# Softplus from ScalarE's softplus table instead of abs, exp, ln and four VectorE operations, in a linear attention followed by a softplus MLP

## The chip, the cores and the metric

One core of one Trainium2 chip. The core has TensorE (PE, with weight loads shown apart as PEld), VectorE (DVE), ScalarE (ACT), GpSimd (POOL) and SyncE (SP, which only issues DMAs here). Each engine takes its instructions in the order of its own queue; semaphores order the engines against each other. The metric is the time on the device in microseconds (us), the median of several runs.

## The reference

```
kv  = einsum('bhsd,bhse->bhde', k, v)            # 8 batches, 8 heads, 576 tokens, 64 features
out = einsum('bhsd,bhde->bhse', q, kv)
rms = sqrt(mean(out * out, axis=-1) + 1e-06)
x   = (out / rms * g_norm), as 4608 tokens x 512 features
h   = x @ w_in                                   # 512 x 2048
g   = maximum(h, 0) + log1p(exp(-abs(h)))        # softplus
y   = g @ w_out                                  # 2048 x 512, float32
```

q, k and v are float32. w_in and w_out come as float64 and are rounded to float32 on the core.

## The kernel before

The tokens are worked in 12 blocks of 384. A block has 16 slots, one for each 128 of the 2048 hidden features; slots are counted on through the blocks here, so slot 16 is the first of block 1. What a slot holds is written out by hand, and each engine's queue has that order.

*mm1* (lines 236 to 258), once per slot: four float32 matmuls into a PSUM tile hp of 128x384, then softplus into g, the block's tile of hidden activations. There are two hp buffers, so the hp of a slot can start when the softplus two slots earlier has read its hp for the last time. The softplus is three ScalarE operations (L249 Abs, L250 Exp, L252 Ln) and four VectorE operations (L254, L255, L256, L257). L256 is the last that reads hp; L257 writes g.

*mm2* (262 to 273), in 12 of the 16 slots of the next block: a quarter (four matmuls) of op = g^T w_out for 128 tokens; after the last quarter ScalarE copies the result out and it is stored.

*The attention* of batch b is dealt over slots. stage_turn (171) has the transposes of q (tp), which ScalarE (L187) and VectorE (L189) copy out, and the product kv (L192), copied by L194 and L195. stage_out (203) forms o, its squares on ScalarE (L211) and x times g_norm on VectorE (L212). stage_squares (215) sums the squares by a matmul (ss), which VectorE brings to ms (L220). stage_root (223) is one ScalarE square root per batch, with a load of ScalarE's table ahead of it and another after it (L225). stage_norm (227), eight per batch, is a VectorE reciprocal (L229) and a product (L231). All PSUM tiles of the attention come from one pool of four buffers.

*The conversion* of the weights (convert, 119) goes in 32 chunks, each a 128x512 piece: 16 of w_in, then 16 of w_out. Six are converted during the first batch, 26 in slots 0 to 15, one or two per slot. A chunk takes one ScalarE operation (L132, c_lf), five on VectorE (L133 c_h, L134 and L136 c_t, L138 c_p, L141 c_m) and four on GpSimd (L139 c_m from c_h, L143, L144 and L147, tensor-tensor operations, the last of which writes the weight). VectorE's L141 waits for GpSimd's L139 of the same chunk, and GpSimd's L139 waits for VectorE's L133. The buffers between them are double, so c_lf of a chunk waits until GpSimd has done with the chunk two before it.

*Order in a slot.* In slots 0 to 15 each engine's queue has the slot's mm1 with its softplus first, then the attention of batch 1 that falls on the slot, then the slot's conversion. Batch 1 has its turns, outs and squares in slots 0 to 8, its root in slot 8 and one norm in each of slots 8 to 15. From slot 16 on, the later batches' attention stands between mm1 and mm2.

*Memory.* The conversion's buffers are given back after block 0, and the second g tile (g1, for the odd blocks) is placed there (lines 312 to 315). So the first write of g1, in slot 16, waits for the end of the conversion.

Of the kernel before, what the change touches and what calls it, by code (L numbers as in the profile page):

```python
# [8 lines left out]
F32 = mybir.dt.float32  # L9
U32 = mybir.dt.uint32  # L10
AF = mybir.ActivationFunctionType
ALU = mybir.AluOpType
PSUM = bass.MemoryType.PSUM

P = 128
# [4 lines left out]
def kernel(  # L20
# [7 lines left out]
    moe_w_out: bass.AP,  # L28
    out: bass.AP,
):  # L30
    """Per batch and pair of heads: kv = k^T v, x^T = kv^T q^T (features on partitions, so that it is
    the moving operand of the next product), the mean of squares over a head by a product with a
    block of ones, which leaves it on every row of the head. Then per block of NT tokens:
    g = softplus(w_in^T x^T), out = g^T w_out. Products and sums are float32; weights that come as
    float64 (their bits in 64-bit integers) are rounded to it here. The attention of the batches
    ahead is dealt out over the slots of the block products."""
    nc = tc.nc
    B, H, S, D = q.shape
    d_model, d_ff = moe_w_in.shape
    n_tokens = out.shape[0]  # L40
    assert (B, H, S, D, d_model) == (8, 8, 576, 64, 512) and n_tokens == B * S
    NP = H // 2                      # pairs of heads
    KD, KF = d_model // P, d_ff // P
    J = 6                            # tokens on one partition of q, k and v
    R = S // J                       # partitions of q, k and v
    HS = S // 2                      # half of a batch's tokens: one bank of PSUM
    JH = J // 2
    NT = 384                         # tokens of a block
    SLOTS = KF
    GB = 2                           # batches whose x^T lies in one tile  # L50
    BPT = GB * S // NT               # blocks of such a tile
    n_blocks = n_tokens // NT

    ctx.enter_context(tc.manual_schedule())
# [12 lines left out]
    block = const.tile([P, P], F32, name="block")  # L67
# [5 lines left out]
    def load(u):  # L73
        if u >= B * NP:
            return
        b, p = divmod(u, NP)
        tiles = []
        for n, src in (("q", q), ("k", k), ("v", v)):
            # q and k are stationary operands: the pair's 128 features lie together for each j
            t = qkv.tile([R, 2, J, D] if n == "v" else [R, J, 2, D], F32, tag=n, name=f"{n}_t")  # L80
            pair = src[b, 2 * p:2 * p + 2].rearrange("h (r j) d -> r h j d", j=J)
            if n == "v":
                nc.sync.dma_start(out=t, in_=pair)
            else:
                for e in range(2):
                    nc.sync.dma_start(out=t[:, :, e], in_=pair[:, e])
            tiles.append(t)
        loaded[u] = tiles
# [3 lines left out]
    conv_pool = tc.tile_pool(name="conv", bufs=2)  # L92
    conv = conv_pool.__enter__()
    raws = {}
    CHUNKS = 2 * KF                  # a weight's columns (w_in) or rows (w_out) of one kf

    def weight(c):
        """DRAM and SBUF views of chunk c, d_model values on a partition."""
        kf = c % KF
        if c < KF:  # L100
            words = moe_w_in.bitcast(U32) if wide else moe_w_in
            n = words.shape[1] // KF
            return (words[:, kf * n:(kf + 1) * n].rearrange("(a p) f -> p a f", p=P),
                    w_in_t[:, :, kf * P:(kf + 1) * P])
        words = moe_w_out.bitcast(U32) if wide else moe_w_out
        return words[kf * P:(kf + 1) * P].rearrange("(a p) f -> p a f", p=P), w_out_t[:, kf:kf + 1]
# [10 lines left out]
            out=raws[c].rearrange("p n two -> p (n two)").rearrange("p (a f) -> p a f", a=src.shape[1]), in_=src)  # L117

    def convert(c):
        """float64 -> float32, from the words hi (sign, exponent, 20 bits of mantissa) and lo.  # L120

        t: hi's value in float32: the exponent's top bit and its low seven stay, the three between
        only tell the range. p: t's power of two with its sign. So the value is t + lo 2^-52 p,
        which one addition rounds. m is 1 inside float32's normal range, 0 below it, huge above."""
        if not wide:
            return
        raw = raws.pop(c)
        lo, hi = raw[:, :, 0], raw[:, :, 1]
        t, p, h = (conv.tile([P, d_model], U32, tag=n, name=f"c_{n}") for n in "tph")
        lf, m = (conv.tile([P, d_model], F32, tag=n, name=f"c_{n}") for n in ("lf", "m"))  # L130
        tf, pf = t.bitcast(F32), p.bitcast(F32)
        nc.scalar.activation(lf, lo, func=AF.Copy, scale=2.0 ** -52)  # L132
        nc.vector.tensor_scalar(out=h, in0=hi, scalar1=0x7FFFFFFF, scalar2=None, op0=ALU.bitwise_and)  # L133
        nc.vector.tensor_scalar(out=t, in0=hi, scalar1=3, scalar2=0x3FFFFFF8,  # L134
                                op0=ALU.logical_shift_left, op1=ALU.bitwise_and)
        nc.vector.scalar_tensor_tensor(out=t, in0=hi, scalar=0xC0000000, in1=t,  # L136
                                       op0=ALU.bitwise_and, op1=ALU.bitwise_or)
        nc.vector.tensor_scalar(out=p, in0=t, scalar1=0xFF800000, scalar2=None, op0=ALU.bitwise_and)  # L138
        nc.gpsimd.tensor_scalar(out=m, in0=h, scalar1=float((1023 + 128) << 20), scalar2=3e38,  # L139
                                op0=ALU.is_ge, op1=ALU.mult)  # L140
        nc.vector.scalar_tensor_tensor(out=m, in0=h, scalar=float((1023 - 126) << 20), in1=m,  # L141
                                       op0=ALU.is_ge, op1=ALU.add)
        nc.gpsimd.tensor_tensor(out=lf, in0=lf, in1=pf, op=ALU.mult)  # L143
        nc.gpsimd.tensor_tensor(out=lf, in0=lf, in1=tf, op=ALU.add)  # L144
        _, dst = weight(c)
        a = dst.shape[1]
        nc.gpsimd.tensor_tensor(out=dst, in0=lf.rearrange("p (a f) -> p a f", a=a),  # L147
                                in1=m.rearrange("p (a f) -> p a f", a=a), op=ALU.mult)
        fetch(c + 3)
# [5 lines left out]
    for c in range(3 if wide else CHUNKS):  # L155
        fetch(c)

    nc.scalar.preload_act_table_set("natural_log_exp_and_others")
    ln_one = const.tile([P, 1], F32, name="ln_one")
    nc.vector.memset(ln_one, 0.0)  # L160
    nc.scalar.activation(ln_one, ln_one, func=AF.Ln, bias=1.0)
    make_identity(nc, ident)
    for t in [block] + kv_diag:
        nc.vector.memset(t, 0.0)
# [4 lines left out]
    qTs, sqs = {}, {}  # L169

    def stage_turn(u):
        """q^T and the block-diagonal kv of a pair of heads."""
        b, p = divmod(u, NP)
        if p == 0:
            mss[b] = att.tile([P, 2, NP, HS], F32, tag="ms", bufs=1, name="ms")
# [25 lines left out]
        return xTs[b // GB][:, p, c:c + HS]  # L201

    def stage_out(u):
        """The attention's rows times g, and their squares."""
        b, p = divmod(u, NP)
        qT = qTs.pop(u)
        for h in range(2):
# [14 lines left out]

    def stage_root(b):
        nc.scalar.activation(mss[b], mss[b], func=AF.Sqrt)  # L224
        nc.scalar.preload_act_table_set("natural_log_exp_and_others")  # L225

    def stage_norm(b, h, p):
        r = mss[b][:, h, p]
# [7 lines left out]
    def mm1(n, kf):  # L236
# [5 lines left out]
        for kd in range(KD):  # L242
            nc.tensor.matmul(hp, lhsT=w_in_t[:, kd, kf * P:(kf + 1) * P], rhs=xT[:, kd, c:c + NT],  # L243
                             start=(kd == 0), stop=(kd == KD - 1))
        # softplus(h) = max(h, 0) + log1p(u), u = exp(-|h|);
        # log1p(u) = ln(w) + (u - (w - 1)) with w = 1 + u rounded, which keeps small u whole
        # once what the table gives for ln(1) is taken off.
        u = tmp.tile([P, NT], F32, tag="u", name="u")
        nc.scalar.activation(u, hp, func=AF.Abs)  # L249
        nc.scalar.activation(u, u, func=AF.Exp, scale=-1.0)  # L250
        ln = tmp.tile([P, NT], F32, tag="ln", name="ln")
        nc.scalar.activation(ln, u, func=AF.Ln, bias=1.0)  # L252
        w = tmp.tile([P, NT], F32, tag="w", name="w")
        nc.vector.tensor_scalar(out=w, in0=u, scalar1=1.0, scalar2=None, op0=ALU.add)  # L254
        nc.vector.scalar_tensor_tensor(out=w, in0=w, scalar=1.0, in1=u, op0=ALU.subtract, op1=ALU.subtract)  # L255
        nc.vector.scalar_tensor_tensor(out=ln, in0=hp, scalar=0.0, in1=ln, op0=ALU.max, op1=ALU.add)  # L256
        nc.vector.scalar_tensor_tensor(out=gs[n][:, kf], in0=ln, scalar=ln_one, in1=w,  # L257
                                       op0=ALU.subtract, op1=ALU.subtract)

    PARTS = 4                        # slots over which one tile of 128 tokens is summed  # L260

    def mm2(n, i, part):
        if part == 0:
# [8 lines left out]
            r0 = n * NT + i * P  # L272
            nc.sync.dma_start(out=out[r0:r0 + P], in_=ot)

    # the first batch
    for t in range(NP + 2):
        if t < NP:
            stage_turn(t)
# [7 lines left out]
        for p in range(NP):  # L286
            stage_norm(0, h, p)

    # the other batches, by slot
    agenda = {}  # L290

    def at(slot, f, *a):
        agenda.setdefault(slot, []).append((f, a))

    for b in range(1, B):
        # the slot where the first block that takes from batch b starts, less the slots of its work
        due = (b * S // NT) * SLOTS
        s0 = max(due - (28 if b % GB else 30), 0)
        for p in range(NP):
# [4 lines left out]
        for i in range(2 * NP):  # L304
            at(s0 + 2 * NP + (i + 1 if b > 1 else i), stage_norm, b, i // NP, i % NP)

    AHEAD = NP + 2                   # chunks of the weights that are ready before the first block
    for c in range(AHEAD, CHUNKS):
        at((c - AHEAD) * SLOTS // (CHUNKS - AHEAD), convert, c)

# [44 lines left out]
```

## Time and profile before

| | us |
|---|---|
| median of 3 runs (lowest, highest) | 1355.65 (1354.22, 1356.6) |
| profiled execution, span | 1353.7 |
| PE busy in the span | 1166.8 (86%) |
| VectorE busy | 775.3 (57%) |
| ScalarE busy | 418.8 (31%) |
| GpSimd busy | 214.2 (16%) |

The page of the profile gives each engine's busy time in 40 equal slices, in tenths, and the clock that PE was granted (PEclk, in tenths of full speed). A row of the timeline gives the start, the duration in us, the engine, the line, the operation with its output and inputs, and in brackets how long the engine stood idle before it and which operation ended that wait. A row of the waits gives who waited for whom, us in total, the number of times and the longest. The lines are those of the kernel before.

### The profile page before, as it was taken

What the parts mean: (1) busy time and instruction counts of PE and PEld (TensorE: products, weight loads), DVE (VectorE), ACT (ScalarE), POOL (GpSimd) and SP (SyncE); (2) the same over time, 40 slices, a digit from 0 to 9 for tenths busy, and PEclk for the clock granted to TensorE, in tenths of its full rate; (3) what the DMA queues carried; (4) which work ended last, traced back from release to release, by engine and by line L of the source; (5) the groups of instructions that cost most, each with busy time, mean ns of one, the idle gap of its engine ahead of it and who ended that gap; (6) DMA issues with size and microseconds to landing.
All of it is one profiled execution on the core that took longest, in us unless ns stands there. A gap on an engine that the chain in (4) does not pass through costs nothing.

```text
span 1353.7 us, 10306 instructions
## 1 busy us (share of the span) xinstructions
PE 1166.8 (86%) x3520; PEld 642.1 (47%) x3520; DVE 775.3 (57%) x1254; ACT 418.8 (31%) x798; POOL 214.2 (16%) x134
## 2 busy tenths in 40 slices
PE   6164524259999999999999999999999999999998
PEld 4042312125555555555555555555555555555543
DVE  4888989885384476343674584335844754343320
ACT  2222222113433343333432433334233333233320
POOL 5658776770000000000000000000000000000000
PEclk8667766579999999999999999999999999999999
DMA  9324311102202200012012100121020000000000
GB/s 212 86 73 115 89 62 46 62 16 66 55 8 61 61 8 8 16 46 68 16 35 60 35 9 8 30 65 35 8 61 9 8 16 9 8 8 8 16 8 24
DMA packets 98582, 55.21 MB, mean 41 GB/s; under 512 B 77536, under 2 KB 91872, under 8 KB 98528
## 3 DMA queue, kind: packets, MB, share of 16 engines
q1 hardware_dynamic: 98528, 54.54, 14.9%
q8 instruction: 28, 0.46, 0.1%
q14 instruction: 26, 0.21, 0.0%
HBM read 45.09 MB, written 9.44 MB: 40 GB/s over the span
## 4 chain that ended last, share of the span: by engine, by line
PE 76%; DVE 10%; POOL 8%; ACT 3%; issue 1%; DMA 1%; SPq 1%; POOLq 0%; ACTq 0%
PE op L267 36%; PE hp L243 34%; POOL c_m L139 4%; PE kv L192 3%; DVE ms L229 2%; PE o L209 2%; DVE w L255 2%; DVE w L254 2%; POOL c_lf L143 2%; POOL c_lf L144 1%; DVE g L257 1%; DVE c_m L141 1%; ACT qT L187 1%; ACT u L250 1%; ACT u L249 1%
## 5 line engine op out<-in xcount | busy, mean ns | idle before, releaser
L243 PE MATMUL hp<-xT,w_in_t 128*128 128x384 f32 x1536 | 550.7, 507 | 111.3 <-DVE ln L256 85.2
L267 PE MATMUL op<-w_out_t,g 128*128 128x512 f32 x1152 | 516.1, 592 | 0.0
L243 PEld LDWEIGHTS hp<-xT,w_in_t 128*128 128x128 f32 x1536 | 303.7, 199 | 358.4 <-issue 98.6
L254 DVE TENSOR_SCALAR w<-u 128x384 f32<-128x384 f32 x192 | 85.9, 448 | 468.1 <-ACT u L250 468.1
L267 PEld LDWEIGHTS op<-w_out_t,g 128*128 128x128 f32 x1152 | 217.0, 190 | 238.1 <-issue 211.9
L249 ACT ACTIVATE u<-hp 128x384 f32<-128x384 f32 x192 | 93.9, 489 | 580.5 <-PE hp L243 580.4
L257 DVE SCALAR_TENSOR_TENSOR g<-ln,ln_one,w 128x384 f32<-128x384 f32 x192 | 124.9, 650 | 14.5 <-POOL w_out_t L147 0.7
L255 DVE SCALAR_TENSOR_TENSOR w<-w,u 128x384 f32<-128x384 f32 x192 | 122.3, 637 | 6.7
L229 DVE RECIPROCAL ms<-ms 128x288 f32<-128x288 f32 x64 | 124.5, 1945 | 2.2 <-ACT ms L224 2.2
L256 DVE SCALAR_TENSOR_TENSOR ln<-hp,ln 128x384 f32<-128x384 f32 x192 | 105.9, 551 | 0.9
L252 ACT ACTIVATE ln<-u 128x384 f32<-128x384 f32 x192 | 100.5, 524 | 6.1
L250 ACT ACTIVATE u<-u 128x384 f32<-128x384 f32 x192 | 100.4, 523 | 6.1
L139 POOL TENSOR_SCALAR c_m<-c_h 128x512 f32<-128x512 uint32 x32 | 70.4, 2201 | 81.7 <-DVE c_h L133 80.6
L192 PE MATMUL kv<-v_t,k_t 96*128 96x128 f32 x384 | 58.7, 310 | 21.6 <-ACT qT L187 16.2
L192 PEld LDWEIGHTS kv<-v_t,k_t 96*128 96x128 f32 x384 | 52.7, 217 | 26.6 <-ACT qT L187 20.6
L132 ACT ACTIVATE c_lf<-raw 128x512 f32<-128x512 uint32 x32 | 21.2, 667 | 127.3 <-POOL w_out_t L147 84.7
L209 PE MATMUL o<-qT,kv_diag 128*128 128x288 f32 x128 | 40.8, 445 | 21.1 <-DVE kv_diag L195 20.4
L143 POOL TENSOR_TENSOR c_lf<-c_lf,c_p 128x512 f32<-128x512 f32 x32 | 56.5, 1767 | 2.6
L271 ACT COPY ot<-op 128x512 f32<-128x512 f32 x36 | 21.1, 586 | 109.1 <-PE op L267 109.1
L184 PE MATMUL tp<-ident,q_t 96*128 96x96 f32 x192 | 24.3, 266 | 24.9 <-DVE xT L212 18.9
L209 PEld LDWEIGHTS o<-qT,kv_diag 128*128 128x128 f32 x128 | 25.8, 207 | 34.1 <-DVE kv_diag L195 22.3
L219 PE MATMUL ss<-sq,block 128*128 128x288 f32 x128 | 37.7, 419 | 4.4 <-DVE xT L212 2.9
(33 smaller groups left out, 469.9 us busy)
## 6 DMA issues: line engine op xcount, KB each, us to landing
q_t<-in_q_dram SPq DMA_DIRECT2D x64, 144.0 KB, 3.1
k_t<-in_k_dram SPq DMA_DIRECT2D x64, 144.0 KB, 3.5
v_t<-in_v_dram SPq DMA_DIRECT2D x32, 288.0 KB, 3.8
out_dram<-ot SPq DMA_DIRECT2D x36, 256.0 KB, 2.0
raw<-in_moe_w_in_dram SPq DMA_DIRECT2D x16, 512.0 KB, 4.1
raw<-in_moe_w_out_dram SPq DMA_DIRECT2D x16, 512.0 KB, 3.3
g_col<-in_g_norm_dram SPq DMA_DIRECT2D x2, 0.2 KB, 3.1
```

Source lines behind the costliest of these rows:

```text
L139: nc.gpsimd.tensor_scalar(out=m, in0=h, scalar1=float((1023 + 128) << 20), scalar2=3e38, op0=ALU.is_ge, op1=ALU.mult)
L192: nc.tensor.matmul(kv, lhsT=k_t[:, j].rearrange("r h d -> r (h d)"), rhs=v_t[:, :, j, :], start=(j == 0), stop=(j == J - 1))
L229: nc.vector.reciprocal(r, r)
L243: nc.tensor.matmul(hp, lhsT=w_in_t[:, kd, kf * P:(kf + 1) * P], rhs=xT[:, kd, c:c + NT], start=(kd == 0), stop=(kd == KD - 1))
L249: nc.scalar.activation(u, hp, func=AF.Abs)
L250: nc.scalar.activation(u, u, func=AF.Exp, scale=-1.0)
L252: nc.scalar.activation(ln, u, func=AF.Ln, bias=1.0)
L254: nc.vector.tensor_scalar(out=w, in0=u, scalar1=1.0, scalar2=None, op0=ALU.add)
L255: nc.vector.scalar_tensor_tensor(out=w, in0=w, scalar=1.0, in1=u, op0=ALU.subtract, op1=ALU.subtract)
L256: nc.vector.scalar_tensor_tensor(out=ln, in0=hp, scalar=0.0, in1=ln, op0=ALU.max, op1=ALU.add)
L257: nc.vector.scalar_tensor_tensor(out=gs[n][:, kf], in0=ln, scalar=ln_one, in1=w, op0=ALU.subtract, op1=ALU.subtract)
L267: nc.tensor.matmul(op, lhsT=gs[n][:, kf, i * P:(i + 1) * P], rhs=w_out_t[:, kf], start=(kf == 0), stop=(kf == KF - 1))
```

## The change

The three ScalarE and four VectorE operations become one ScalarE ACTIVATE with the function Softplus, which reads hp and writes g. ScalarE's preloaded table set becomes the one of softplus, loaded after each batch's root; the preload at the start goes, with ln_one (the table's value of ln(1), which L257 subtracted). Comments are removed too, so that line numbers shift (L249 becomes L241, L192 becomes L188).

```
-    nc.scalar.preload_act_table_set("natural_log_exp_and_others")
-    ln_one = const.tile([P, 1], F32, name="ln_one")
-    nc.vector.memset(ln_one, 0.0)
-    nc.scalar.activation(ln_one, ln_one, func=AF.Ln, bias=1.0)
...
         nc.scalar.activation(mss[b], mss[b], func=AF.Sqrt)
-        nc.scalar.preload_act_table_set("natural_log_exp_and_others")
+        nc.scalar.preload_act_table_set("softplus")
...
-        u = tmp.tile([P, NT], F32, tag="u", name="u")
-        nc.scalar.activation(u, hp, func=AF.Abs)
-        nc.scalar.activation(u, u, func=AF.Exp, scale=-1.0)
-        ln = tmp.tile([P, NT], F32, tag="ln", name="ln")
-        nc.scalar.activation(ln, u, func=AF.Ln, bias=1.0)
-        w = tmp.tile([P, NT], F32, tag="w", name="w")
-        nc.vector.tensor_scalar(out=w, in0=u, scalar1=1.0, scalar2=None, op0=ALU.add)
-        nc.vector.scalar_tensor_tensor(out=w, in0=w, scalar=1.0, in1=u, op0=ALU.subtract, op1=ALU.subtract)
-        nc.vector.scalar_tensor_tensor(out=ln, in0=hp, scalar=0.0, in1=ln, op0=ALU.max, op1=ALU.add)
-        nc.vector.scalar_tensor_tensor(out=gs[n][:, kf], in0=ln, scalar=ln_one, in1=w,
-                                       op0=ALU.subtract, op1=ALU.subtract)
+        nc.scalar.activation(gs[n][:, kf], hp, func=AF.Softplus)
```

What this does to the queues shows at three places. A row is one instruction in the order of its engine; in brackets stand the engines and DMA queues whose semaphores it waits for. The first is VectorE's queue late in block 0, from the last operation of one slot's conversion to the first of the next slot's, before (L254 to L257 are the softplus, L229 and L231 the norm):

```order
L141 SCALAR_TENSOR_TENSOR c_m<-c_h,c_m 128x512 [waits Pool_49]
L254 TENSOR_SCALAR w<-u 128x384 [waits Activation_49]
L255 SCALAR_TENSOR_TENSOR w<-w,u 128x384 [waits DVE_49]
L256 SCALAR_TENSOR_TENSOR ln<-hp,ln 128x384 [waits Activation_49]
L257 SCALAR_TENSOR_TENSOR g_128<-ln,ln_one,w 128x384 [waits DVE_49]
L229 RECIPROCAL ms<-ms 128x288
L231 TENSOR_TENSOR xT<-xT,ms 128x288 [waits DVE_49]
L133 TENSOR_SCALAR c_h<-raw 128x512 [waits DMAHW1_49]
```

and now:

```order
L141 SCALAR_TENSOR_TENSOR c_m<-c_h,c_m 128x512 [waits Pool_49]
L225 RECIPROCAL ms<-ms 128x288
L227 TENSOR_TENSOR xT<-xT,ms 128x288 [waits DVE_49]
L133 TENSOR_SCALAR c_h<-raw 128x512 [waits DMAHW1_49]
L134 TENSOR_SCALAR c_t<-raw 128x512
```

The softplus is gone from between the two chunks; the norm and c_h follow directly.

The second place is the end of the conversion (slots 15 to 17). VectorE's queue before, where g_1302 is g1:

```order
L141 SCALAR_TENSOR_TENSOR c_m<-c_h,c_m 128x512 [waits Pool_49]
L254 TENSOR_SCALAR w<-u 128x384 [waits Activation_49]
L255 SCALAR_TENSOR_TENSOR w<-w,u 128x384 [waits DVE_49]
L256 SCALAR_TENSOR_TENSOR ln<-hp,ln 128x384 [waits Activation_49]
L257 SCALAR_TENSOR_TENSOR g_1302<-ln,ln_one,w 128x384 [waits DVE_49,Pool_49]
```

and ScalarE's queue now, where g_124 is the first g tile and g_1154 is g1:

```order
L241 ACTIVATE g_124<-hp 128x384 [waits PE_49]
L132 ACTIVATE c_lf<-raw 128x512 [waits DMAHW3_49,Pool_49]
L241 ACTIVATE g_1154<-hp 128x384 [waits PE_49,Activation_49,Pool_49]
L241 ACTIVATE g_1154<-hp 128x384 [waits PE_49] x2
L183 COPY qT<-tp 128x3x96 [waits PE_49]
L190 COPY kv_diag_86<-kv 64x64 [waits PE_49]
```

The wait of the first write of g1 for GpSimd has moved from VectorE's last softplus operation, which no longer held hp, to ScalarE's only one, which reads hp.

The third place is PE's queue in block 1, at the second turn of batch 2 (L219 is ss, L184 tp, L192 kv, L267 op). Before:

```order
L219 MATMUL ss<-sq,block 128x288 [waits Activation_49] x2
L184 MATMUL tp<-ident,q_t 128x96 [waits DMAHW3_49,DMAHW2_49,DVE_49]
L184 MATMUL tp<-ident,q_t 128x96 x2
L184 MATMUL tp<-ident,q_t 128x96 [waits DVE_49]
L184 MATMUL tp<-ident,q_t 128x96 x2
L192 MATMUL kv<-v_t,k_t 128x128 [waits DMAHW5_49,DMAHW6_49,DMAHW4_49,Activation_49]
L192 MATMUL kv<-v_t,k_t 128x128 x5
L267 MATMUL op<-w_out_t,g_128 128x512 [waits Pool_49] x4
```

and now:

```order
L215 MATMUL ss<-sq,block 128x288 [waits Activation_49] x2
L180 MATMUL tp<-ident,q_t 128x96 [waits DMAHW3_49,DMAHW2_49,DVE_49]
L180 MATMUL tp<-ident,q_t 128x96 x2
L180 MATMUL tp<-ident,q_t 128x96 [waits DVE_49]
L180 MATMUL tp<-ident,q_t 128x96 x2
L188 MATMUL kv<-v_t,k_t 128x128 [waits DMAHW5_49,DMAHW6_49,DMAHW4_49,DVE_49]
L188 MATMUL kv<-v_t,k_t 128x128 x5
L250 MATMUL op<-w_out_t,g_124 128x512 [waits Pool_49] x4
```

The buffer that kv gets is another one: its last reader was a ScalarE operation and is now a VectorE operation.

## The prediction

> **What bounds the kernel now.** I read the page first, its 40 slices above all (34 us each), then busy time by stretches, the waits of two stretches, and the timeline at the places where those waits end.
>
> ```profile
> span 1353.7 us, 10306 instructions
> ...
> PE   6164524259999999999999999999999999999998
> ...
> DVE  4888989885384476343674584335844754343320
> ...
> POOL 5658776770000000000000000000000000000000
> PEclk8667766579999999999999999999999999999999
> ```
>
> Two stages differ. Up to slice 9 TensorE (PE) is mostly idle and at a low clock, while VectorE (DVE) is at 80 to 90% and GpSimd (POOL) works; that is where the weights are converted. From slice 10 on PE is full. The two stretches by busy time:
>
> ```profile
> 304.00:1308.80 1004.80, 990.57 (x3057) 542.89 (x3056) 518.19 (x937) 345.29 (x666) 0.05 (x1) 1.00 0.10 29
> 80.00:304.00 224.00, 98.08 (x238) 55.37 (x237) 199.18 (x230) 50.76 (x93) 174.03 (x104) 0.69 0.24 69
> ```
>
> After the length come PE, weight loads, DVE, ScalarE (ACT), POOL, then the clock. In 80:304 PE is busy 98 of 224 us, DVE 199, POOL 174. In 304:1308.8 PE is idle for 1004.80 - 990.57 = 14.23 us only: there softplus costs nothing except through those 14 us. Who is waited for, the first row from the stretch 78:308, the second from 308:1354:
>
> ```profile
> POOL c_m L139 <- DVE c_h L133: 64.6, 16, 21.7
> ...
> PE kv L192 <- ACT qT L187: 14.2, 18, 0.8
> ```
>
> So POOL waits for DVE's first step of a chunk, and the 14.2 us are 18 waits of PE for one ScalarE copy. The first and the last step of POOL's 26 chunks in the slots, and what PE and DVE do there:
>
> ```profile
> 80.01 2.18 POOL L139 TENSOR_SCALAR c_m<-c_h 128x512 f32<-128x512 uint32 x1 [21.67 <-DVE c_h L133]
> ...
> 302.56 1.49 POOL L147 TENSOR_TENSOR w_out_t<-c_lf,c_m 128x512 f32<-128x512 f32 x1
> ...
> 303.42 2.85 PE L243 MATMUL hp<-xT,w_in_t 128*128 128x384 f32 x8 [1.72 <-DVE ln L256]
> ...
> 304.09 0.62 DVE L257 SCALAR_TENSOR_TENSOR g<-ln,ln_one,w 128x384 f32<-128x384 f32 x1 [0.72 <-POOL w_out_t L147]
> ```
>
> The conversion runs from 80.01 to 302.56 + 1.49 = 304.05, which is 224.0 us. Of these POOL waits 64.6 - 21.7 = 42.9 us (the 21.7 lie before its start), in 15 waits; the other 181.1 us are 26 chunks of 6.97 us. The PE row is the hp of slot 18, after which PE stands no more except for the 14.2 us. The time is therefore set by POOL and DVE taking turns until 304, then by PE.
>
> **Where softplus sits in that turn.** One slot near the end, DVE's rows of the timeline and then POOL's:
>
> ```profile
> 289.20 0.69 DVE L141 SCALAR_TENSOR_TENSOR c_m<-c_h,c_m 128x512 f32<-128x512 uint32 x1 [1.06 <-POOL c_m L139]
> 289.81 1.42 DVE L254 TENSOR_SCALAR w<-u 128x384 f32<-128x384 f32 x1
> 291.26 1.50 DVE L255 SCALAR_TENSOR_TENSOR w<-w,u 128x384 f32<-128x384 f32 x1
> ...
> 294.25 1.94 DVE L229 RECIPROCAL ms<-ms 128x288 f32<-128x288 f32 x1
> 296.23 0.46 DVE L231 TENSOR_TENSOR xT<-xT,ms 128x288 f32<-128x288 f32 x1
> 296.60 0.42 DVE L133 TENSOR_SCALAR c_h<-raw 128x512 uint32<-128x512 uint32 x1
> ```
>
> ```profile
> 289.24 1.76 POOL L143 TENSOR_TENSOR c_lf<-c_lf,c_p 128x512 f32<-128x512 f32 x1
> 291.09 1.26 POOL L144 TENSOR_TENSOR c_lf<-c_lf,c_t 128x512 f32<-128x512 f32 x1
> 292.43 1.49 POOL L147 TENSOR_TENSOR w_out_t<-c_lf,c_m 128x512 f32<-128x512 f32 x1
> 297.11 2.18 POOL L139 TENSOR_SCALAR c_m<-c_h 128x512 f32<-128x512 uint32 x1 [3.20 <-DVE c_h L133]
> ```
>
> The four softplus operations hold DVE from 289.81 to 294.25, 4.44 us. Only then come the norm and the next c_h, while POOL, free at 293.92, waits 3.20 us. The rows also show that DVE operations beside POOL's tensor-tensor work are long: L254 1.42 us here. The next rows show what of the rest of DVE's work suffers, in the first batch and in the first slots:
>
> ```profile
> 53.77 1.77 POOL L143 TENSOR_TENSOR c_lf<-c_lf,c_p 128x512 f32<-128x512 f32 x1
> 54.34 1.94 DVE L229 RECIPROCAL ms<-ms 128x288 f32<-128x288 f32 x1
> ...
> 56.31 0.88 DVE L231 TENSOR_TENSOR xT<-xT,ms 128x288 f32<-128x288 f32 x1
> ...
> 82.83 1.50 DVE L133 TENSOR_SCALAR c_h<-raw 128x512 uint32<-128x512 uint32 x1
> ...
> 84.12 1.33 POOL L144 TENSOR_TENSOR c_lf<-c_lf,c_t 128x512 f32<-128x512 f32 x1
> ...
> 86.97 2.25 POOL L139 TENSOR_SCALAR c_m<-c_h 128x512 f32<-128x512 uint32 x1
> ```
>
> The reciprocal beside POOL takes the 1.94 us that it takes alone. The product L231 takes 0.88 for 0.46; c_h takes 1.50 for 0.42 and ends at 84.33, 0.2 us into POOL's next operation. The last row has no wait: two chunks without softplus between them follow each other at 86.97 - 80.01 = 6.96 us, POOL never idle.
>
> **The sum, against the profiled execution.** Its span is 1353.7; the median of the runs is 1355.65, 1.95 above.
>
> (1) *POOL's waits.* In an ordinary slot c_h comes 4.44 us earlier for DVE, more than POOL's wait plus what c_h loses by running beside POOL (1.50 - 0.42 = 1.08). With a norm ahead of it: reciprocal from 289.81 to 291.76, the product ends with L144 (292.35) plus about 0.3, c_h ends with L147 (293.92) plus about 0.3 = 294.2, POOL starts 0.1 later, 0.3 us after it could. That is 7 slots, 2.1 us. The first norm of the batch waits for the root, in slot 8:
>
> ```profile
> 185.28 0.81 DVE L220 TENSOR_SCALAR ms<-ss 128x288 f32<-128x288 f32 x2
> ...
> 191.16 2.18 POOL L139 TENSOR_SCALAR c_m<-c_h 128x512 f32<-128x512 uint32 x1 [6.21 <-DVE c_h L133]
> ```
>
> From ms to POOL's next start are 191.16 - 185.28 = 5.88 us, ScalarE's root among them. Begun 4.44 us earlier, at 180.84, this gives 186.72; POOL was free 6.21 before its row, with its usual gap of 0.1 at 185.0: 1.7 us. So 3.8 us of waits stay of 42.9, and the conversion ends at 304.05 - 39.1 = 264.9.
>
> (2) *A wait moves to ScalarE.* g of block 1 lies where the conversion's buffers were, and the row at 304.09 shows g of slot 16 waiting for POOL's last step. Behind that wait stood only DVE; PE's buffer had been freed by L256 before it. Now the one ScalarE operation that frees the buffer writes g, so it starts at 264.9, and all of ScalarE's queue stands behind it: softplus 17, later the copies of batch 2. PE's hp of slot 18 follows it. A softplus from PSUM is not in the trace; the nearest row is Abs from the same buffer, 0.49 us (below), the far bound 1.6 us, all three old operations. With 0.49 and some 0.05 at each hand-over, PE starts at 265.5 instead of 303.42: -37.9 us. Were it not for that wait, softplus 16 would stand only behind the c_lf of the last chunk, which waits for the chunk two before: two periods, 14 us earlier.
>
> (3) *A cold start.* PE will have stood there for some 9 us (softplus 15 stands behind the c_lf of chunk 30, which waits for chunk 28, so it comes three chunks, 21 us, before the end; hp 17 and two parts of op fill about 12 of them). The first row is eight matmuls after such a wait, the second without one:
>
> ```profile
> 293.29 4.99 PE L243 MATMUL hp<-xT,w_in_t 128*128 128x384 f32 x8 [8.69 <-DVE ln L256]
> ...
> 314.95 2.74 PE L243 MATMUL hp<-xT,w_in_t 128*128 128x384 f32 x8
> ```
>
> The difference is +2.3 us, or nothing if PE is kept busy. The Trainium skill (TensorE: Matmul & The Clock Gate, Part 1: The HAM clock gate) has half clock for about 3.4 us after an idle window; by it the loss would be 1.7 us, and the sum 0.6 lower.
>
> (4) *PE's 18 waits later on.* One of them, PE's rows and ScalarE's:
>
> ```profile
> 318.50 0.66 PE L184 MATMUL tp<-ident,q_t 96*128 96x96 f32 x6
> 319.96 1.60 PE L192 MATMUL kv<-v_t,k_t 96*128 96x128 f32 x12 [0.80 <-ACT qT L187]
> ```
>
> ```profile
> 317.74 0.49 ACT L249 ACTIVATE u<-hp 128x384 f32<-128x384 f32 x1 [1.35 <-PE hp L243]
> ...
> 318.81 0.53 ACT L252 ACTIVATE ln<-u 128x384 f32<-128x384 f32 x1
> 319.25 0.67 ACT L187 COPY qT<-tp 128x288 f32<-128x288 f32 x1
> ```
>
> The copy comes late because Abs, Exp and Ln are ahead of it. In the new order of instructions kv waits for a DVE operation instead, by its place the one that empties ss. That one can start when ss is done, before tp ends at 319.16, since DVE has no softplus to finish. I take all 14.2 us; if the old wait stayed, the copy would start at about 318.9 and save some 0.3 each, 6 us.
>
> (5) *At nothing:* the first table load and ln_one (the start is set by loads and PE), the loads per root (as many as before), the last block's tail, which is PE's op alone.
>
> Sum: 1353.7 - 37.9 + 2.3 - 14.2 = 1303.9; plus 1.95, **1306 us**.
>
> **The rivals.** *(A) POOL is held up by more.* In step (1) DVE always has work ready when a POOL operation ends. L143, which starts just behind DVE's c_m, takes 1.77 us where L144, the same form, takes 1.26. If the two other tensor-tensor operations of each chunk lost such 0.5 us, 26 us would come back: 1332. Against it stand the row at 84.12, 1.33 beside a ready c_h, and the period of 6.96. Its milder form, one more us in each slot, is 16 us: 1322. Chance 0.18. The Trainium skill (SBUF — State Buffer, Who interferes with whom) states the harder form: VectorE and GpSimd share a port pair that goes whole to whoever starts first, and the other is blocked to the end of that instruction.
>
> *(B) kv still waits* for something behind ScalarE: 1306 + 8 = 1314, at most 1320. For it: the order shows who is waited for, not how long. Chance 0.17.
>
> *(C) Slower: the softplus operation is long.* In 304:1308.8 there are 176 slots of 1004.8 / 176 = 5.7 us. ScalarE is busy 345.3 us there, some 270 of them with the three old operations, so 0.4 us of a slot are other work. A softplus over 5.3 us would set the pace; to eat the gain of 50 us it needs 5.6, eleven times Abs, and at 7 us the time would be about 1306 + 176 x 1.7 = 1605. Nothing speaks for it: the old operations, three different functions, differ by 0.04 us. Chance 0.03.
>
> *(D) The change does not reach the bound:* ScalarE's queue, with c_lf waiting for POOL ahead of each softplus, holds PE, PE holds DVE, and POOL waits as before; 1356. Against it: the c_lf of a chunk waits only for the chunk two before. Chance 0.02.
>
> **How the numbers follow.** Forecast 0.60, A 0.18, B 0.17, C 0.03, D 0.02. Low end: no waits left (-3.8), no cold start (-2.3), POOL's L144 always at 1.26 instead of 1.33 (26 x 0.07, -2): 1298. High end: B at its worst and some of A, 1322. Above it lie the harder part of A, C and D, about 0.15. A measurement of this kernel tells 0.2%, 2.7 us, from no change: faster 0.95, same 0.02, slower 0.03.
>
> **What would show it.** Right: POOL's waits in the slots near 4 us, its last step near 265, one ScalarE operation of about 0.5 us per slot, the one of slot 16 starting as POOL ends, PE without waits from then on. Wrong: POOL periods over 7.2 us beside DVE work (A), kv with idle time ahead of it (B), softplus over 2 us (C).

## The result, and the profile after

| | before | after |
|---|---|---|
| median (lowest, highest), us | 1355.32 (1354.22, 1356.6) | 1299.83 (1298.96, 1301.22) |
| profiled execution, span, us | 1353.7 | 1297.4 |

The ratio is 0.9591 (95% interval 0.9577 to 0.9604): 55.5 us less. The forecast was 1306 in a range of 1298 to 1322, so it was 6.2 us too high. The median of before has a fourth run in it now. These are the same rows of the page as were shown of before:

```profile
span 1297.4 us, 8783 instructions
...
PE   6166633489999999999999999999999999999998
...
DVE  4878879811602600014212500126015100000000
...
POOL 5759989900000000000000000000000000000000
PEclk9667766789999999999999999999999999999999
```

A slice is now 32 us, and the first digit is slice 1. GpSimd (POOL) is at 80% or more from slice 4 on and done after slice 8; before, it was at 60 to 80% there and lasted through slice 9. VectorE (DVE) is busy for less than a tenth of whole slices later on, and PE is full from slice 10. Busy time of the two stretches, in the order PE, weight loads, DVE, ScalarE (ACT), POOL, then the clock:

```profile
78.00:264.00 186.00, 95.14 (x239) 54.83 (x238) 155.34 (x169) 33.52 (x60) 171.86 (x104) 0.71 0.28 83
264.00:1297.00 1033.00, 1029.78 (x3152) 560.96 (x3150) 180.42 (x240) 174.78 (x324) 0.00 (x0) 1.00 0.10 28
```

In the conversion POOL is busy 172 of 186 us, where it was 174 of 224. POOL does the same work with less waiting. The waits of the changed kernel, the first two rows from 78:265, the last from 262:1297:

```profile
POOL c_m L139 <- DVE c_h L133: 26.1, 9, 21.5
...
ACT g L241 <- POOL w_out_t L147: 13.3, 1, 13.3
...
PE hp L239 <- ACT g L241: 11.8, 1, 11.8
```

Of POOL's 26.1 us, 21.5 lie before its start, so 4.6 us are left of the 42.9 us in the slots. In the rows of the second stretch PE's matmuls wait once, at its beginning; the 18 waits of kv for ScalarE are gone. POOL's timeline has the first of the 26 chunks, the one that waits for the batch's root, one of the seven that wait for a norm, and the last step:

```profile
78.57 2.19 POOL L139 TENSOR_SCALAR c_m<-c_h 128x512 f32<-128x512 uint32 x1 [21.48 <-DVE c_h L133]
...
170.68 2.19 POOL L139 TENSOR_SCALAR c_m<-c_h 128x512 f32<-128x512 uint32 x1 [1.98 <-DVE c_h L133]
...
255.89 2.18 POOL L139 TENSOR_SCALAR c_m<-c_h 128x512 f32<-128x512 uint32 x1 [0.37 <-DVE c_h L133]
...
261.34 1.26 POOL L147 TENSOR_TENSOR w_out_t<-c_lf,c_m 128x512 f32<-128x512 f32 x1
```

The conversion runs from 78.57 to 261.34 + 1.26 = 262.60, that is 184.0 us where it took 224.0. At its end stand ScalarE's softplus of slots 16 and 17 and PE's hp of slot 18:

```profile
262.64 0.87 ACT L241 ACTIVATE g<-hp 128x384 f32<-128x384 f32 x2 [13.33 <-POOL w_out_t L147]
263.18 5.37 PE L239 MATMUL hp<-xT,w_in_t 128*128 128x384 f32 x8 [11.78 <-ACT g L241]
```

ScalarE starts 0.04 us after POOL's last step, and PE follows ScalarE. The wait has moved as forecast, and PE comes out of it with eight matmuls that take 5.37 us instead of 2.85.

### The profile page after: what moved, and what is told of

The parts are those of the page before. It is cut to its first block, busy times and chain, and to the rows that moved or that the text cites. A ratio compares the mean times of both kernels' runs of the same rounds, so it can differ in the third digit from the quotient of the medians.

```text
span 1297.4 us, 8783 instructions
## 1 busy us (share of the span) xinstructions
PE 1161.2 (89%) x3520; PEld 641.4 (49%) x3520; DVE 388.9 (30%) x485; ACT 226.2 (17%) x413; POOL 211.8 (16%) x134
## 4 chain that ended last, share of the span: by engine, by line
PE 80%; POOL 11%; DVE 5%; issue 2%; SPq 1%; DMA 0%; ACT 0%; POOLq 0%; ACTq 0%
PE op L250 38%; PE hp L239 35%; POOL c_m L139 4%; PE kv L188 3%; POOL c_lf L143 3%; DVE ms L225 2%; POOL c_lf L144 2%; PE o L205 2%; PE ss L215 2%; POOL w_in_t L147 1%; PE tp L180 1%; DVE c_h L133 1%; DVE xT L227 1%; POOL w_out_t L147 1%; DVE c_m L141 1%
## 5 line engine op out<-in xcount | busy, mean ns | idle before, releaser
L241 ACT ACTIVATE g<-hp 128x384 f32<-128x384 f32 x192 | 94.0, 490 | 717.2 <-PE hp L239 703.8
L185 DVE COPY qT<-tp 128x288 f32<-128x288 f32 x32 | 21.6, 676 | 291.1 <-PE tp L180 290.3
L208 DVE TENSOR_SCALAR xT<-o,g_col 128x288 f32<-128x288 f32 x64 | 32.2, 517 | 159.5 <-ACT sq L207 158.8
L188 PE MATMUL kv<-v_t,k_t 96*128 96x128 f32 x384 | 58.4, 311 | 12.7 <-ACT qT L183 8.3
L188 PEld LDWEIGHTS kv<-v_t,k_t 96*128 96x128 f32 x384 | 53.8, 222 | 14.5 <-ACT qT L183 9.3
L143 POOL TENSOR_TENSOR c_lf<-c_lf,c_p 128x512 f32<-128x512 f32 x32 | 56.7, 1771 | 2.6
L216 DVE TENSOR_SCALAR ms<-ss 128x288 f32<-128x288 f32 x64 | 28.5, 456 | 91.2 <-PE ss L215 90.6
L254 ACT COPY ot<-op 128x512 f32<-128x512 f32 x36 | 21.1, 586 | 139.4 <-PE op L250 139.4
L144 POOL TENSOR_TENSOR c_lf<-c_lf,c_t 128x512 f32<-128x512 f32 x32 | 41.4, 1294 | 2.5
L136 DVE SCALAR_TENSOR_TENSOR c_t<-raw,c_t 128x512 uint32<-128x512 uint32 x32 | 41.2, 1286 | 1.1
L180 PE MATMUL tp<-ident,q_t 96*128 96x96 f32 x192 | 24.6, 270 | 17.5 <-DVE xT L208 11.4
L133 DVE TENSOR_SCALAR c_h<-raw 128x512 uint32<-128x512 uint32 x32 | 36.0, 1125 | 3.4 <-DMA raw<-in_moe_w_in_dram 3.2
```

Source lines behind the costliest of these rows:

```text
L188: nc.tensor.matmul(kv, lhsT=k_t[:, j].rearrange("r h d -> r (h d)"), rhs=v_t[:, :, j, :], start=(j == 0), stop=(j == J - 1))
L241: nc.scalar.activation(gs[n][:, kf], hp, func=AF.Softplus)
```

## The experiments

The theory, T: the gain has two parts that do not touch each other. VectorE is free sooner in slots 0 to 15 and so POOL waits less (some 40 us, less the cold start); and kv no longer waits for ScalarE's copy behind the old softplus, worth more than the 14.2 us of PE's idle time. The rivals: the second part is only those 14.2 us, or the gain comes from ScalarE's shorter work. In e4, e5, e9 and e10 the added operations write what nothing reads.

**e1 and e2: each part alone.** e1 has the one operation in block 0 and the old seven from block 1 on; e2 is the reverse. Both keep the old start, and the table sets are loaded to match.

```
-        nc.scalar.activation(gs[n][:, kf], hp, func=AF.Softplus)
+        if n == 0:                       # e2: if n > 0
+            nc.scalar.activation(gs[n][:, kf], hp, func=AF.Softplus)
+            return
+        u = tmp.tile([P, NT], F32, tag="u", name="u")
...
```

> Only the 16 slots of block 0 use the one-operation softplus; from slot 16 on the seven old operations stand again. Theory T (the gain of about 56 us is two separate parts: GpSimd no longer waits for VectorE while the weights are converted, about 38 us net of the cold start, and kv no longer waits behind ScalarE, 18 times 1.04 = 18.7 us): this kernel has the first part alone, conversion over near 263 us, kv waits of 0.8 us still there, about 1318 us. Rival R (the gain comes from the shorter chain in every slot, so it is spread over the slots): 16 of 192 slots bring a twelfth, about 1351 us.

> The seven old operations in block 0, the one-operation softplus from slot 16 on. Theory T: the conversion ends near 304 us as before, and only the 18 waits of kv go, 18.7 us: about 1336 us. If the idle time that the waits showed (14.2 us) is all that they cost: about 1341 us. Rival R (spread over the slots): eleven twelfths of the gain, about 1304 us.

e1 took 1317.66 us (1316.72 to 1318.68), ratio 0.9718 (0.9703 to 0.9732); e2 took 1339.43 us (1338.85 to 1339.92), ratio 0.9878 (0.9863 to 0.9893); before on the same chip took 1356.09. The gains are 38.4 and 16.7 us, together 55.1, and the whole change brought 55.5: two parts that add up. In e1 PE's hp of slot 18, a kv later on, and the row of its waits in 262:1315:

```profile
263.21 4.27 PE L243 MATMUL hp<-xT,w_in_t 128*128 128x384 f32 x8 [10.71 <-DVE ln L256]
...
281.18 1.60 PE L192 MATMUL kv<-v_t,k_t 96*128 96x128 f32 x12 [0.80 <-ACT qT L187]
...
PE kv L192 <- ACT qT L187: 14.3, 18, 0.8
```

PE's hp of slot 18 starts as early as in the changed kernel, though POOL's last step ends 1.2 us later (263.81), and the 18 waits stay. In e2 it is the other way: POOL waits as before, and the hp of slot 18 starts where it did.

```profile
POOL c_m L139 <- DVE c_h L133: 64.6, 16, 21.7
...
303.89 4.54 PE L243 MATMUL hp<-xT,w_in_t 128*128 128x384 f32 x8 [2.45 <-ACT g L246]
```

e2 lies between the two forecasts, nearer to the lower price. The row shows why: the forecast by T left out that the wait for POOL had moved to ScalarE there too. The hp starts 303.89 - 303.42 = 0.5 us later than before and takes 4.54 - 2.85 = 1.7 us longer. e2's span is 1337.5, which is 16.2 less; with those 2.2 us the waits themselves were worth 18.4, not 14.2.

**e4 and e5: whose relief is it?** e4 puts ScalarE's two other operations back, e5 VectorE's four in block 0:

```
 e4, ahead of the Softplus
+        u = tmp.tile([P, NT], F32, tag="u", name="u")
+        nc.scalar.activation(u, hp, func=AF.Square)
+        nc.scalar.activation(u, u, func=AF.Square)
 e5, behind it
+        if n > 0:
+            return
+        g = gs[n][:, kf]
...
+        nc.vector.tensor_scalar(out=w, in0=g, scalar1=1.0, scalar2=None, op0=ALU.add)
+        nc.vector.scalar_tensor_tensor(out=w, in0=w, scalar=1.0, in1=g, op0=ALU.subtract, op1=ALU.subtract)
+        nc.vector.scalar_tensor_tensor(out=ln, in0=hp, scalar=0.0, in1=g, op0=ALU.max, op1=ALU.add)
+        nc.vector.scalar_tensor_tensor(out=ln, in0=ln, scalar=1.0, in1=w, op0=ALU.subtract, op1=ALU.subtract)
```

> The changed kernel with two more ScalarE operations ahead of each softplus (squares of hp into a tile that nothing else reads), so that ScalarE has three operations per slot as before and VectorE none. Theory T: only VectorE's four operations mattered for the conversion, and kv waits for VectorE, not for ScalarE; about 1301 us (1 us for the longer softplus of slot 16 at the end of the conversion). Rival R (ScalarE's shorter chain brings the gain): about 1340 us or more.

> The changed kernel with four VectorE operations after the softplus of each slot of block 0, of the old ones' forms (one on g, one on two tiles in SBUF, one that reads hp, one on two tiles), whose results nothing else reads. ScalarE keeps its one operation. Theory T: GpSimd waits for VectorE again by some 43 us in 15 waits, the conversion ends near 302 us, and the time is about 1339 us. Rival R (ScalarE's shorter chain brings the gain): about 1300 us.

e4 took 1299.38 us (1298.99 to 1301.21), ratio 0.9587 (0.9571 to 0.9603): the same as the changed kernel. In its ScalarE rows of a slot the three operations are there:

```profile
704.54 0.49 ACT L242 ACTIVATE u<-hp 128x384 f32<-128x384 f32 x1 [5.81 <-PE hp L239]
705.06 0.52 ACT L243 ACTIVATE u<-u 128x384 f32<-128x384 f32 x1
705.49 0.47 ACT L244 ACTIVATE g<-hp 128x384 f32<-128x384 f32 x1
```

ScalarE works three times as long on a softplus and PE waits no more than in the changed kernel: in this slot ScalarE had idled for 5.81 us ahead of them. e5 took 1338.13 us (1337.56 to 1338.66), ratio 0.987 (0.9856 to 0.9885), against 1355.75 of before on that chip; its POOL row of the waits reads

```profile
POOL c_m L139 <- DVE c_h L133: 64.6, 16, 21.7
```

which is before's, word for word. Four VectorE operations in the 16 slots of block 0 take back 38.3 us of the gain (1338.13 - 1299.83, measured on two chips). So the first part is VectorE's relief. For the second e4 says that three ScalarE operations do no harm while VectorE is free of softplus, although in the prediction they were what made the copy late.

**e9 and e10: why kv waited.** e9 has VectorE's four operations in blocks 1 to 11 and not in block 0; e10 has ScalarE's two Squares there as well.

```
 e9, as e5 but
-        if n > 0:
+        if n == 0:
             return
 e10, as e9 and ahead of the Softplus
+        if n > 0:
+            u = tmp.tile([P, NT], F32, tag="u", name="u")
+            nc.scalar.activation(u, hp, func=AF.Square)
+            nc.scalar.activation(u, u, func=AF.Square)
```

> The changed kernel with VectorE's four old operations back behind the Softplus in blocks 1 to 11 (they write what nothing reads); ScalarE keeps its one operation. Theory T: the kv waits went because VectorE, free of softplus, empties ss before tp has ended, so that kv can take the buffer of ss; with the four operations back kv takes a buffer that ScalarE's copy of tp empties, as before, and waits again. The copy is not behind Abs, Exp and Ln now: in the changed kernel it ends at 281.24 + 0.68 = 281.92, 0.63 us after kv starts at 281.29, so each of 18 kv comes some 0.65 to 0.75 us later: 1299.8 + 12 to 13.5, some 1313. The conversion ends as in the changed kernel. Rival S, the waits went because ScalarE's queue got shorter: no waits, 1300.

> The same, and ahead of the Softplus in blocks 1 to 11 two ScalarE Squares as well, so that both engines have their old load from block 1 on. Theory T: the copy stands behind three ScalarE operations again, so all of the second part is given back: 1299.8 + 18 x 1.04 = 1318.5, as with the old seven operations there (1317.7). If kv waits were cheaper than I take them (14.2 in all): 1314. Rival S, ScalarE's load alone decides: already excluded if the kernel with ScalarE's Squares alone stood at 1299.4, so then 1300 here too only if neither load matters.

e9 took 1314.7 us (1314.42 to 1315.28), ratio 0.9695 (0.968 to 0.9709); e10 took 1316.34 us (1314.78 to 1317.71), ratio 0.9706 (0.969 to 0.9722), both against 1356.23. e9's hp of slot 18 and, from 262 to its end, PE's and the weight loads' waits for the copy; then the same waits of e10:

```profile
265.91 4.69 PE L239 MATMUL hp<-xT,w_in_t 128*128 128x384 f32 x8 [13.19 <-DVE ln L249]
...
PEld kv L188 <- ACT qT L183: 12.6, 18, 0.7
PE kv L188 <- ACT qT L183: 9.3, 18, 0.5
```

```profile
PEld kv L188 <- ACT qT L183: 14.3, 18, 0.8
PE kv L188 <- ACT qT L183: 11.0, 18, 0.6
```

All 18 waits for ScalarE's copy are back in e9, though ScalarE has its one operation. kv does not read what the copy writes, so it waits for the buffer that the copy empties: with VectorE's operations in the program, kv is given that buffer again. Rival S is out. VectorE now comes to ss only after kv has started:

```profile
284.01 1.60 PE L188 MATMUL kv<-v_t,k_t 96*128 96x128 f32 x12 [0.52 <-ACT qT L183]
...
284.52 0.81 DVE L216 TENSOR_SCALAR ms<-ss 128x288 f32<-128x288 f32 x2
```

Which buffer kv gets is fixed in the order of instructions, before anything runs. VectorE's load therefore acts through that choice, and no run here keeps the buffer and changes the load alone.

e9's span is 1313.1, 15.7 more than the changed kernel's; 2.0 of that come at slot 18, whose hp starts 265.91 - 263.18 = 2.7 us later and is 0.7 shorter, which the expectation left out, and 13.7 are the waits. Of the 2.7 us, 1.3 are there from the start of the conversion's slots (79.85 against 78.57); the rest is the hp's wait for VectorE. ScalarE's load sets only how long the wait is: e10's span is 1314.4, and its waits, worked out in the same way, cost 15.3. That is below the 18.6 of before, so all was not given back as its Theory T had it; its two Squares and the Softplus let the copy begin some 0.2 us sooner after tp than Abs, Exp and Ln did (rows below), and 18 times 0.2 is 3.6. The runs of e9 and e10 overlap, so the difference between them rests on the two profiles.

Where the copy begins in e10, PE's tp and then ScalarE's copy:

```profile
282.49 0.66 PE L180 MATMUL tp<-ident,q_t 96*128 96x96 f32 x6
...
283.04 0.66 ACT L183 COPY qT<-tp 128x288 f32<-128x288 f32 x1
```

That is 0.55 us after tp's start, where it was 319.25 - 318.50 = 0.75 before.

**e3: the moved wait.** The first four tiles of g1 lie in memory of their own, so that softplus of slots 16 to 19 need not wait for POOL:

```
+    EARLY = 4
+    g_early = const.tile([P, EARLY, NT], F32, name="g_early")
...
-            g_tiles.append(late.tile([P, KF, NT], F32, name="g1"))
+            g_tiles.append(late.tile([P, KF - EARLY, NT], F32, name="g1"))
```

> The changed kernel, with the first four slots of the odd blocks' g in a small tile of their own, so that the softplus of slots 16 to 19 no longer waits for the end of the conversion. Theory T: that wait stands on the path, PE's hp of slot 18 starts two conversion periods earlier (near 249 instead of 263 us), and the stretch up to the first part of op that needs the last chunk (19.5 us after hp 18 in the changed kernel) moves ahead of the conversion's end: some 13 us less, about 1287 us. Rival W (PE then waits for the last chunk or for batch 2's copies on VectorE, which stand behind the last chunk's conversion): at most 4 us less, about 1296 us.

e3 took 1284.78 us (1284.3 to 1285.55), ratio 0.9475 (0.9461 to 0.949), faster than both kernels. PE's op ahead of the hp of slot 18, and that hp:

```profile
247.61 3.60 PE L255 MATMUL op<-w_out_t,g 128*128 128x512 f32 x8
251.05 2.74 PE L244 MATMUL hp<-xT,w_in_t 128*128 128x384 f32 x8
```

It starts 263.18 - 251.05 = 12.1 us sooner, with no wait, and takes 5.37 - 2.74 = 2.6 us less. Together that is 14.7 us, which is the whole difference of the spans (1297.4 - 1282.7). The moved wait cost the change 14.7 us.

**e6: the old start.** The conversion's slots began at 78.57 instead of 80.01, which no step of the prediction had. e6 puts the old table load, ln_one and its Ln back at the start of the changed kernel.

```
+    nc.scalar.preload_act_table_set("natural_log_exp_and_others")
+    ln_one = const.tile([P, 1], F32, name="ln_one")
+    nc.vector.memset(ln_one, 0.0)
+    nc.scalar.activation(ln_one, ln_one, func=AF.Ln, bias=1.0)
```

> The changed kernel with the removed lines at the start put back (a load of the old table set, the memset and the ln of one value, which nothing else reads). Theory S (these lines, or the buffers that PE's second and third kv get because of them, cost the first batch 1.4 us): the first chunk in the slots starts on GpSimd near 80.0 us as in the kernel before, and the time is about 1301 us. Rival N (the 1.4 us are chance of one execution): it starts near 78.6 us, 1300 us.

It took 1299.64 us (1298.94 to 1300.01), ratio 0.9585 (0.9569 to 0.9601): no different from the changed kernel. Its first chunk in the slots:

```profile
79.15 2.18 POOL L139 TENSOR_SCALAR c_m<-c_h 128x512 f32<-128x512 uint32 x1 [21.32 <-DVE c_h L133]
```

That is 0.6 us later than 78.57 and 0.9 earlier than 80.01, in one profile of each. The other profiles spread as widely: without the old lines this chunk starts at 78.44 (e3), 78.46 (e4), 79.33 (e5), 79.41 (e10) and 79.85 (e9), with them at 79.35 (e1) and 79.69 (e2). So neither the 1.4 us nor a part of it can be put down to these lines, and in the time none of it can be told. Where it comes from stays open.

**e7: what bounds it next.** If POOL sets the time up to slot 18, work for POOL in the stretch where it has none should bring more. e7 is e3 with eight chunks more in the first batch, one after each of its norms, and so eight fewer in the slots.

```
+            convert(NP + 2 + h * NP + p)          # after stage_norm(0, h, p)
...
-    AHEAD = NP + 2
+    AHEAD = NP + 2 + 2 * NP
```

> The kernel with the first four slots of g apart (e3), and eight more chunks converted ahead of block 0, one after each of the eight norms of batch 0; 18 chunks are left for the slots. Theory T (with the softplus off VectorE the first stage is set by GpSimd's queue, which in the changed kernel stands 21.5 us before the slots while VectorE makes those norms): GpSimd waits some 0.4 us per norm instead, the conversion ends about 17 us earlier, near 245 us, and the time is about 1268 us. Rival P (with one chunk per slot TensorE or VectorE set the slots of batch 1 instead): the conversion ends after 255 us, 1278 us or more.

e7 took 1263.97 us (1263.56 to 1264.94), ratio 0.9329 (0.9313 to 0.9344), against 1354.75 of before on that chip, some 4 us under the forecast. POOL's last step, and PE's rows up to the hp of slot 18:

```profile
243.18 1.27 POOL L147 TENSOR_TENSOR w_out_t<-c_lf,c_m 128x512 f32<-128x512 f32 x1
```

```profile
216.91 5.33 PE L244 MATMUL hp<-xT,w_in_t 128*128 128x384 f32 x8 [4.26 <-ACT g L246]
222.07 3.60 PE L255 MATMUL op<-w_out_t,g 128*128 128x512 f32 x8
225.50 2.74 PE L244 MATMUL hp<-xT,w_in_t 128*128 128x384 f32 x8
228.08 3.60 PE L255 MATMUL op<-w_out_t,g 128*128 128x512 f32 x8
231.52 2.74 PE L244 MATMUL hp<-xT,w_in_t 128*128 128x384 f32 x8
```

The conversion ends at 244.45, as expected, and 18.1 us before e3's (262.52), where 17 had been forecast; rival P is out. The hp of slot 18 starts 251.05 - 231.52 = 19.5 us before e3's, which is the difference of the spans (1282.7 - 1263.2). PE stands no more from 216.91 on, 27 us before POOL is done: the conversion's end alone no longer says when PE is full.

## Why the prediction was right, and where it was off

**(1) POOL's waits: right.** Of 42.9 us, 4.6 stayed; the forecast was 3.8. The seven norm slots cost 0.37 each (0.3 forecast) and the root 1.98 (1.7 forecast). A norm slot, rows of VectorE and POOL between one chunk and the next:

```profile
251.54 1.95 DVE L225 RECIPROCAL ms<-ms 128x288 f32<-128x288 f32 x1
252.82 1.26 POOL L144 TENSOR_TENSOR c_lf<-c_lf,c_t 128x512 f32<-128x512 f32 x1
253.52 0.88 DVE L227 TENSOR_TENSOR xT<-xT,ms 128x288 f32<-128x288 f32 x1
254.16 1.36 POOL L147 TENSOR_TENSOR w_out_t<-c_lf,c_m 128x512 f32<-128x512 f32 x1
254.32 1.48 DVE L133 TENSOR_SCALAR c_h<-raw 128x512 uint32<-128x512 uint32 x1
```

This is the chain as it was worked out: the product ends just after L144 (254.40 after 254.08), c_h just after L147 (255.80 after 255.52). Two smaller terms came out lower. A chunk without waits takes (184.0 - 4.6) / 26 = 6.90 us, not 6.97, which is 1.7 us in all; and the start was 1.4 us earlier, which no run puts down to the change (e6). With the 0.8 us more of waits the conversion ended 2.3 us before the 264.9 forecast.

**(2) The wait that moves to ScalarE: right.** From POOL's end to PE's hp were 0.58 us; the forecast was 0.6. For "two periods, 14 us earlier" without that wait, e3's hp started 12.1 us earlier, and with the cold start the whole was 14.7. The softplus that had no row in the trace took what Abs takes:

```profile
L241 ACT ACTIVATE g<-hp 128x384 f32<-128x384 f32 x192 | 94.0, 490 | 717.2 <-PE hp L239 703.8
```

**(3) The cold start: right, its size in part by luck.** PE stood 11.8 us and not some 9: hp 17 (5.48 us) and only one quarter of op (3.63) lay between, where the prediction had two. The first hp then took 5.37 us, against before's own 2.85 at this place, so 2.5 us more; the forecast was 2.3. The measured cost is not one number: e1's hp, after 10.71 us, took 4.27, which is 1.4 more than 2.85, and e2's, after only 2.45 us, took 4.54, 1.7 more. The granted clock, the third number from the end, says why. These are busy times during that hp in the changed kernel, in e1 and in e2:

```profile
263.18:268.38 5.20, 5.20 (x8) 2.75 (x9) 0.00 (x0) 0.33 (x1) 0.00 (x0) 0.51 0.00 0
...
263.21:267.31 4.10, 4.10 (x8) 2.32 (x9) 2.54 (x5) 0.00 (x0) 0.61 (x1) 0.65 0.00 0
...
303.89:308.27 4.38, 4.38 (x9) 2.38 (x10) 0.00 (x0) 0.33 (x1) 0.00 (x0) 0.61 0.00 0
```

In before's own hp, 303.42:306.11, the clock was 1.00. In the changed kernel it was 0.50 in 263.2:267.8 and 1.00 in 268.4:269.0. Counting each hp as part at 0.50 and part at 1.00, the means give an estimate of 5.1 us at half clock in the changed kernel, 2.9 in e1 and 3.4 in e2; half of each is the 2.5, 1.4 and 1.7 us lost. By the Trainium skill (TensorE: Matmul & The Clock Gate, Part 1: The HAM clock gate), with half clock for about 3.4 us, the estimate was 1.7: e2 agrees with it, and in the changed kernel the half clock lasted longer.

**(4) The 18 waits of kv: the mechanism was right, the term was mis-sized.** "I take all 14.2 us" was the failing step. From hp of slot 18 to the end the kernel took 1353.7 - 303.42 = 1050.3 us before and 1297.4 - 263.18 = 1034.2 after, 16.1 less; with the 2.5 of the cold start the waits gave 18.6. The place that the prediction showed, in the changed kernel:

```profile
280.50 0.94 DVE L216 TENSOR_SCALAR ms<-ss 128x288 f32<-128x288 f32 x2 [2.10 <-PE ss L215]
280.79 0.66 PE L180 MATMUL tp<-ident,q_t 96*128 96x96 f32 x6
...
281.29 1.53 PE L188 MATMUL kv<-v_t,k_t 96*128 96x128 f32 x12
...
282.65 1.88 PE L250 MATMUL op<-w_out_t,g 128*128 128x512 f32 x4
```

VectorE begins to empty the two ss at 280.50, before tp starts, and kv follows tp at once, as forecast; by e9 it is VectorE's freedom that does it, through the buffer that kv is given. From tp to the op behind kv are 282.65 - 280.79 = 1.86 us, start to start (the rows of op end with the stretch asked for). Before, that op and the weight loads' row of the waits in 308:1354 were

```profile
321.40 1.88 PE L267 MATMUL op<-w_out_t,g 128*128 128x512 f32 x4
...
PEld kv L192 <- ACT qT L187: 17.5, 18, 1.0
```

so 321.40 - 318.50 = 2.90 us, 1.04 more, and 18 times that is 18.7. From tp's start to kv's it was 1.46 us and is 0.50 now: a wait of 0.96. PE's idle time shows only 0.80 of it, because tp's row, whose end is modelled, reaches 0.16 us past the point at which kv starts when it needn't wait; and kv itself took 1.60 instead of 1.53. The weight loads' row, 17.5 us, had been the better price, and it was there to be read.

**(5) Nothing for the rest: not contradicted.** e6 shows no difference in the time.

**The rivals.** A did not happen: beside a ready c_h POOL lost next to nothing.

```profile
81.40 1.49 DVE L133 TENSOR_SCALAR c_h<-raw 128x512 uint32<-128x512 uint32 x1
82.69 1.33 POOL L144 TENSOR_TENSOR c_lf<-c_lf,c_t 128x512 f32<-128x512 f32 x1
```

c_h starts beside POOL's L143, takes 1.49 us for 0.42 and ends at 82.89, 0.2 us into L144, which takes 1.33 instead of 1.26. The Trainium skill (SBUF — State Buffer, Who interferes with whom) says that when VectorE in a 2-port mode and GpSimd meet, the one that issues first has the shared port pair for its whole instruction and the other is blocked. VectorE's side of these rows agrees with that; which mode c_h ran in, no run here shows. POOL gave up only 0.07 us to a ready VectorE operation, where the harder form of A had 0.5, so the time was 1299.8 and not 1332. B did not happen: no kv waits. C did not happen: the softplus took 490 ns. D did not happen: the conversion ended near the forecast, and e5, which puts only VectorE's four operations back into block 0, brings POOL's waits back.

The sum of the misses, against the span of 1303.9 forecast: 2.3 less by the conversion's end (1.4 of them the earlier start, which is not shown to belong to the change), 4.4 less by kv (18.6 for 14.2), 0.2 more by the cold start, which gives 1297.4, as measured.

## What to carry to other kernels

When two engines take turns on a chain, work that one of them does between two turns makes the other wait, for as much of it as the other cannot cover (in the slot shown, 3.20 us of softplus's 4.44): look for the operations that stand between the last step of one turn and the first of the next, and price them by the other engine's waits in that stage, not by shares of the span. When such a wait goes, follow who writes first into memory that the finished stage gives back: here that kept back 14.7 us beside the 55.5 gained, and four tiles of separate memory won them. Price a wait of PE by the distance between the starts of the operations around it, or by the row of the weight loads: the idle time shown ahead of a matmul was 0.79 us of 1.04.

## What the runs showed of the hardware that was not expected

A reciprocal on VectorE beside POOL's tensor-tensor work takes 1.95 us, as long as alone (1.94), while c_h and the product are stretched (1.48 for 0.42, 0.88 for 0.46) until just after the POOL operation ends. PE's first eight matmuls after a stand of 2.45 us or more at this place cost between 1.4 and 2.5 us more than the 2.85 of before, and the cost does not follow the length of the last stand: 10.71 us of it gave 4.27 (e1), 2.45 us gave 4.54 (e2). It follows the time that the clock stays at half, by estimate 2.9 us in e1, 3.4 in e2 and 5.1 in the changed kernel.
